# Keys of two tiles from centred rows, five more tiles transposed by DMA, and a new order of all instructions

## The chip, the cores and the metric

One Trainium2 chip, one of its cores. A core has TensorE (matmuls; in the profile PE, and its weight loads PEld), VectorE (DVE), ScalarE (ACT), GpSimd (POOL) and a queue for transfers, SyncE (SP). Each engine works through its own instructions in the order in which they were written; engines wait for each other through semaphores. The metric is the time of one execution on the device in microseconds (us); the kernel before takes 169.91 us, the median of three runs (169.8 to 170.13).

## The reference

A linear attention block and a feed-forward block, each behind a layer norm, on x of 2048 rows and 512 columns in bf16; 32 heads of 16 columns; the hidden layer of the second block has 1792 columns.

```python
phi = lambda t: where(t > 0, t + 1, exp(t)) + 1e-6
q, k, v = heads(layernorm(x) @ wqkv)
kv  = einsum("bhsd,bhse->bhde", phi(k), v)
z   = einsum("bhsd->bhd", phi(k))
o   = einsum("bhqd,bhde->bhqe", phi(q), kv) / (einsum("bhqd,bhd->bhq", phi(q), z) + 1e-6)
h   = x + o @ wo
out = h + relu(layernorm(h) @ w1) @ w2
```

The sum over all rows in kv and z is a barrier: no row of o can be had before every key is done.

## The kernel before

The 2048 rows are 16 tiles of 128 rows (t = 0 to 15), and four chunks c of four tiles. The whole program is one list of short words, `ORDER` (line 18): each word is a step, a call of the function `op_<word>` with the numbers behind the dots, and the steps are issued in the order of the list. An engine's own order is the order of its steps in the list, so a step that has to wait holds up everything behind it on its engine. PSUM is eight banks of 128x512 in f32 (`bk`), and each matmul step names the bank that it writes: it can't start before the readers of the bank's last content are done.

*Keys.* `lx` loads x. `S` and `A` take mean and variance of a tile on VectorE, `R` makes the reciprocal deviation on ScalarE (a logarithm and an exponential, lines 232 and 233), `N` normalises the tile on VectorE (line 251, into `ln_nat`, which is `h_nat`). The normalised tile must be transposed for the products: either on TensorE (`T`, line 270, four blocks of 128 columns into a bank, then copied to `lnT` by ScalarE, `E`, or VectorE, `V`), or by a DMA transpose from SP (`X`, line 291). `K` multiplies with wk, four matmuls over the contraction (line 299); `F` is the exponential and `U` the relu of the keys on ScalarE (lines 317 and 320, both from PSUM; one or two tiles at a time), `M` clips the exponential and adds 1e-6 (line 324), `D` adds both (line 327). `W` (line 332) stands for U and D together, on VectorE from PSUM. `G` (line 351) sums phi(k).T times normalised x over all tiles in banks 4 to 7; `za`, `zf` and `z` sum phi(k).

*Middle.* `zc`, `zh` make z ready, `gD` brings the sums out of banks 4 to 7, `kv`, `kx`, `m`, `mA` make from them, wv and wo one matrix for each head block. `Q`, `qF`, `qU`, `qM`, `qD` or `qW` are to queries what K to W are to keys, by chunk. `dn` (line 448) is the denominator, `dnl` and `dnx` (ScalarE) its reciprocal, spread over the columns of each head; `dt` (line 480) transposes it by DMA into `rd`, tile by tile, and `dm` (VectorE) multiplies the queries with it, a chunk at a time. There is a way on TensorE for that too, `rt` and `re`, not used in this list.

*Second half.* `h` (line 494) is o @ wo, `hD` adds x, `s` and `a` are the statistics, `r` the deviation, `n` centres the tile, `x` transposes it by DMA (`t` and `e` on TensorE and ScalarE), `p` (line 510) is the product with w1, `pA` and `pD` its relu on ScalarE and VectorE, `f` (line 530) the product with w2, `fo` (line 538) multiplies with the deviation and adds h, `fd` stores. The deviation of the second norm is applied at the very end, since relu passes a positive factor through. `warm` (line 215) issues dummy matmuls on zeros at the start. `lk`, `lq`, `lv`, `lo`, `l1`, `l2` load weights; `masks` makes constants on GpSimd. All transfers and DMA transposes go through SP.

Of the kernel before, what the change touches and what calls it, by code (L numbers as in the profile page):

```python
# [33 lines left out]
a.3 a.0 hD.2 qM.2.0.2 n.0 a.1 n.1 dm.1.0.2 dm.1.2.2 n.3 s.2 Q.3.2.0 Q.3.3.1 qD.2.0.2 a.2 qM.2.2.2 n.2 qF.3.0.2
qF.3.2.2 l2.3.4 x.0 qM.3.2.2 qD.2.2.2 h.5.6 h.7.7 h.6.5 x.1 t.2.3 r.0.4 e.2 h.4.4 x.3 dn.2.3 dnl.2 dnx.2.0.2
p.0.0.2 dt.8 hD.6 qM.3.0.2 qW.3.2.2 hD.4 p.0.1.3 qD.3.0.2 hD.5 dnx.2.2.2 pA.0.0.2 p.0.3.1 p.0.2.0 dn.3.6
pD.0.2.2 p.0.5.3 p.0.4.2 pD.0.4.2 p.0.7.1 p.0.6.0 p.0.13.3 s.6 dt.10 p.0.12.2 dt.11 dt.9 hD.7 a.6 s.5 dm.2.0.2
dm.2.2.2 dnl.3 pA.0.6.2 a.5 pD.0.12.2 f.2.6.0.7 s.7 h.11.7 h.9.0 p.0.9.3 h.8.5 p.0.8.2 dnx.3.2.2 dnx.3.0.2
# [542 lines left out]
```

## Time and profile before

| | |
|---|---|
| median of three runs | 169.91 us (169.8 to 170.13) |
| span of the profiled execution, first to last instruction | 168.6 us |
| TensorE busy | 163.1 us (97%), 875 matmuls |
| VectorE busy | 104.7 us (62%); 5.00 of 5 us in each slice from 10 to 25 us |
| ScalarE busy | 64.3 us (38%) |
| DMA | 15.36 MB, mean 91 GB/s; 16 engines over 90% busy between 5 and 10 us |

The profiled execution has no time of its own beside its span; the median lies 1.35 us above the span, which is what stands around the first and last instruction. A line `start duration engine line ...` of a timeline gives us from the start of the span. A line of groups gives, behind the count, the busy time and then the mean ns of one instruction. Matmuls are pipelined: a 128x512 matmul of bf16 is written down as 0.38 us, but the next one starts 0.216 us after it, so the end of a group is modelled. `[idle before <-releaser]` says how long the engine had idled and what ended it.

### The profile page before, as it was taken

The page shows a single profiled execution, that of the slowest core. Times are in us where ns is not written, and L with a number is a line of the kernel's source. Part 1 is how long each engine was busy: PE and PEld are TensorE (multiplying, and loading weights), DVE is VectorE, ACT ScalarE, POOL GpSimd, SP SyncE. Part 2 cuts the span into 40 slices and gives each one's busy share as a digit, 9 for nine tenths or more (in the row PEclk, how much of TensorE's full clock was granted, in tenths as well). Part 3 has the DMA queues.
Part 4 walks back from the last instruction along what each step waited for, and adds up shares of the span by engine and source line. Part 5 has one row for each costly group of instructions (what it writes and reads, how often), then busy time and mean ns, then how long its engine had stood idle before and what let it go on. Part 6 is the DMA issues. An engine that isn't in the chain of part 4 may idle for free.

```text
span 168.6 us, 2307 instructions
## 1 busy us (share of the span) xinstructions
PE 163.1 (97%) x875; PEld 76.3 (45%) x875; DVE 104.7 (62%) x207; ACT 64.3 (38%) x97; POOL 4.8 (3%) x21
## 2 busy tenths in 40 slices
...
DMA packets 30091, 15.36 MB, mean 91 GB/s; under 512 B 22656, under 2 KB 29056, under 8 KB 30080
## 3 DMA queue, kind: packets, MB, share of 16 engines
...
HBM read 7.86 MB, written 2.10 MB: 59 GB/s over the span
## 4 chain that ended last, share of the span: by engine, by line
PE 84%; ACT 4%; DMA 4%; SPq 3%; DVE 2%; issue 1%; DVEq 0%; ACTq 0%
PE bk L530 29%; PE bk L510 29%; PE bk L351 7%; PE bk L299 7%; PE bk L494 6%; PE bk L307 5%; DMA wk_sb<-in_A_wqkv_dram 3%; ACT eb L317 1%; DMA rd<-wk_sb 1%; SPq L201 1%; SPq L480 1%; PE bk L448 1%; ACT rb L320 1%; DVE pqT L332 1%; ACT lnT L280 1%
## 5 line engine op out<-in xcount | busy, mean ns | idle before, releaser
L530 PE MATMUL bk<-w_sb,at 128*128 128x512 bf16 (+2 forms) x252 | 51.5, 355 | 0.0
L510 PE MATMUL bk<-lnT,w_sb 128*128 128x512 bf16 x224 | 51.4, 379 | 0.0
L516 ACT ACTIVATE at<-bk 128x1024 bf16<-128x1024 f32 x14 | 14.1, 1023 | 70.3 <-PE bk L510 70.3
L521 DVE TENSOR_SCALAR at<-bk 128x1024 bf16<-128x1024 f32 x14 | 17.0, 1221 | 33.7 <-PE bk L510 33.7
L530 PEld LDWEIGHTS <-at 128*128 128x128 bf16 x252 | 23.6, 98 | 25.2
L510 PEld LDWEIGHTS <-w_sb 128*128 128x128 bf16 x224 | 21.8, 98 | 26.0 <-issue 0.2
L538 DVE SCALAR_TENSOR_TENSOR gT<-bk,rstd,h_nat 128x512 bf16<-128x512 f32 (+2 forms) x18 | 12.0, 686 | 18.3 <-PE bk L530 15.9
L317 ACT ACTIVATE eb<-bk 128x1024 bf16<-128x1024 f32 (+1 forms) x18 | 16.5, 925 | 6.1 <-PE bk L299 3.5
L299 PE MATMUL bk<-wk_sb,lnT 128*128 128x512 bf16 x64 | 15.5, 379 | 0.6 <-DMA wk_sb<-in_A_wqkv_dram 0.5
L494 PE MATMUL bk<-m_sb,pqs 128*128 128x512 bf16 x64 | 15.5, 379 | 0.1
L307 PE MATMUL bk<-lnT,wq_sb 128*128 128x512 bf16 x64 | 15.1, 379 | 0.1
L320 ACT ACTIVATE rb<-bk 128x1024 bf16<-128x1024 f32 (+1 forms) x15 | 13.6, 906 | 1.2 <-PE bk L307 1.2
L351 PE MATMUL bk<-at,h_nat 128*128 128x512 bf16 x56 | 13.7, 379 | 0.0
L500 DVE TENSOR_TENSOR h_nat<-bk,x_nat 128x512 bf16<-128x512 f32 x16 | 10.8, 678 | 2.7 <-PE bk L494 2.6
L226 DVE BATCH_NORM_STATS2 st<-x_nat 128x6 f32<-128x512 bf16 x16 | 10.6, 678 | 1.8 <-DMA x_nat<-in_A_x_dram 1.8
L228 DVE BATCH_NORM_STATS2 st<-h_nat 128x6 f32<-128x512 bf16 x16 | 10.5, 679 | 0.0
L299 PEld LDWEIGHTS <-lnT 128*128 128x128 bf16 x64 | 5.9, 98 | 8.2 <-ACT lnT L280 1.2
L494 PEld LDWEIGHTS <-pqs 128*128 128x128 bf16 x64 | 6.1, 98 | 7.9 <-DVE pqs L484 1.2
L307 PEld LDWEIGHTS <-wq_sb 128*128 128x128 bf16 x64 | 6.1, 97 | 7.3 <-issue 0.4
L351 PEld LDWEIGHTS <-h_nat 128*128 128x128 bf16 x64 | 6.0, 98 | 6.6
L461 ACT ACTIVATE wk_sb<-ld 128x1024 bf16<-128x1024 f32 x8 | 8.0, 1048 | 0.1
L324 DVE TENSOR_SCALAR eb<-eb 128x1024 bf16<-128x1024 bf16 (+1 forms) x18 | 6.9, 388 | 1.2 <-ACT eb L317 1.1
...
## 6 DMA issues: line engine op xcount, KB each, us to landing
...
```

Source lines behind the costliest of these rows:

```text
L299: nc.tensor.matmul(bk[:, b, :], lhsT=lnT[c][:, kd, j * P : (j + 1) * P], rhs=wk_sb[:, kd, :], start=(kd == 0), stop=(kd == KD - 1),)
L307: nc.tensor.matmul(bk[:, b, :], lhsT=wq_sb[:, kd, j * P : (j + 1) * P], rhs=lnT[c][:, kd, :], start=(kd == 0), stop=(kd == KD - 1),)
L317: nc.scalar.activation(out=buf(eb, kind, i, n), in_=bank(at_bank[kind, i], n), func=ACT.Exp)
L320: nc.scalar.activation(out=buf(rb, kind, i, n), in_=bank(at_bank[kind, i], n), func=ACT.Relu)
L351: nc.tensor.matmul(bk[:, KD + kd, :], lhsT=ln_nat[:, t, kd * P : (kd + 1) * P], rhs=pk(t)[:, 0, :], start=(t == 0), stop=(t == NT - 1),)
L494: nc.tensor.matmul(bk[:, b, :], lhsT=pqs[:, (c * KD + jb) % NQ, j * P : (j + 1) * P], rhs=m_sb[:, jb, :], start=(jb == 0), stop=(jb == KD ...
L500: nc.vector.tensor_tensor(out=h_nat[:, t : t + n, :], in0=bank(at_bank["h", t], n), in1=x_nat[:, t : t + n, :], op=ALU.add,)
L510: nc.tensor.matmul(bk[:, b, cols], lhsT=w1_sb[:, kd, f * P : (f + 1) * P], rhs=lnT[c][:, kd, cols], start=(kd == 0), stop=(kd == KD - 1),)
L516: nc.scalar.activation(out=acts[c % 2][:, f : f + n, :], in_=bank(at_bank["p", c, f], n), func=ACT.Relu)
L521: nc.vector.tensor_scalar(out=acts[c % 2][:, f : f + n, :], in0=bank(at_bank["p", c, f], n), scalar1=0.0, scalar2=None, op0=ALU.max,)
L530: nc.tensor.matmul(bk[:, b, 0 : w * P], lhsT=acts[c % 2][:, f, j * P : (j + 1) * P], rhs=w2_sb[:, f, k * P : (k + w) * P], start=(f == 0), ...
L538: nc.vector.scalar_tensor_tensor(out=o_t[:, t % NO, cols], in0=bk[:, at_bank["f", t, k], 0 : w * P], scalar=rstd2[:, t : t + 1], in1=h_nat ...
```

## The change

For tiles 0 and 2 the keys no longer start from the normalised tile. `C` subtracts the mean only, into a new buffer `xc`; `T` transposes that, into `xcT`; `K` multiplies it with wk; and the reciprocal deviation, one number for each row, is applied as the scale of the exponential and the relu (`scale_of`). `Nc` makes the normalised tile from `xc` later, for G and for the queries, and X transposes it by DMA. Tile 0 is transposed, copied and multiplied in two halves of the contraction (tile 2 is transposed in halves, and multiplied whole). `Na` normalises five tiles (1, 6, 7, 8, 13) on ScalarE in place of VectorE; it needs the product -mean x deviation, which `nm` makes on GpSimd. Seven N steps are left out (tiles 0, 1, 2, 6, 7, 8, 13). The tiles transposed by DMA go from nine to fourteen: 0, 1, 2, 5 and 6 come in. The relu and add of tiles 1, 3 and of 14, 15 become W on VectorE, those of the last two query products become U and D. One of the sixteen denominator tiles, tile 5, is transposed on TensorE (`rt.5`, `re.5`). There are seven dummy matmuls, eleven before; the first five transfers are x in place of x and wk mixed; two relu steps of the second half move from ScalarE to VectorE. The list of all steps is new. The change also adds two small constants and steps for another way to sum z (`zg`, `zhi`, `zlo`, `zs`), which the new list doesn't use.

The list at the places that matter, old then new, and the functions:

```diff
-const table lx.0.1 lx.2.1 S.0 lx.1.1 S.2 A.0 S.1 A.2 R.0.1 N.0 R.2.1 lx.3.1 lk.0.2 lx.4.2 masks warm.1.7
-warm.9.7 A.1 R.1.1 T.0.6 S.3 warm.1.7 N.2 T.2.4 N.1 A.3 E.0 R.3.1 T.1.5 lk.2.2 S.4 E.1 N.3 A.4 V.2 S.5 A.5
-K.0.6 lx.6.2 K.1.3 T.3.1 F.0.1 U.0.1 lx.8.4 E.3 K.2.0 M.0.1 S.6 D.0.1 K.3.2 A.6 S.7 F.1.1 M.1.1 lx.12.4 R.4.2
-N.5 A.7 N.4 U.1.1 D.1.1 F.2.1 U.2.1 R.6.2 S.8 S.9 N.7 A.9 A.8 M.2.1 N.6 lq.0.2 G.0 T.5.1 E.5 T.4.3 G.1 X.7
-K.5.1 D.2.1 E.4 K.4.0 R.8.2 T.6.3 G.2 N.9 X.9 F.3.1 U.3.1 S.12 N.8 S.13 X.8 lq.2.2 M.3.1 A.13 A.12 D.3.1 E.6
-K.6.2 F.4.2 R.12.2 U.4.2 K.7.3 G.3 M.4.2 S.11 F.6.2 U.6.2 N.12 D.4.2 S.10 S.14 N.13 M.6.2 A.11 A.10 D.6.2 A.14
-R.10.2 X.12 K.9.1 G.4 N.11 S.15 N.10 A.15 X.13 K.8.0 G.5 G.6 za.2 U.8.2 F.8.2 X.11 X.10 G.7 R.14.2 K.13.1
-K.12.0 M.8.2 N.15 D.8.2 za.4 N.14 K.11.3 K.10.2 G.8 l2.0.3 F.12.2 U.12.2 za.6 X.15 X.14 Q.0.0.0 F.10.2 Q.0.1.1
...
-z.1.2.14 z.3.2.14 qM.0.2.2 l2.7.3 lo.0.2 lo.2.2 l1.2.2 qM.0.0.2 qD.0.2.2 G.13 zc G.14 qD.0.0.2 zh dn.0.0 G.15
-gD.2.2 gD.0.2 Q.1.1.3 Q.1.0.2 dnl.0 dnx.0.0.2 Q.1.2.0 dnx.0.2.2 kv.3.4 kv.0.4 kv.1.4 kv.2.4 Q.1.3.1 qF.1.0.2
-qM.1.0.2 kx qF.1.2.2 qW.1.0.2 dt.0 dt.3 dt.2 dt.1 m.2.6 m.1.5 m.3.7 m.0.4 mA.0.2 Q.2.0.2 Q.2.1.3 qM.1.2.2
-mA.2.2 qW.1.2.2 dn.1.5 dm.0.0.2 dm.0.2.2 dnl.1 dnx.1.2.2 Q.2.3.1 h.3.5 hD.3 h.0.6 h.1.7 hD.0 s.3 dnx.1.0.2
...
-fo.14 fo.15.3.1 f.15.4.0.14.2.1 fd.12 fd.14 fd.15.3.1 fo.15.0.2 fo.15.2.1 fd.15.0.2 fd.15.2.1
+lx.0.1 const table lx.2.1 S.0 lx.3.1 S.2 lx.1.1 A.0 S.3 lx.4.2 R.0.1 A.2 C.0 lk.0.2 R.2.1 A.3 R.3.1 warm.7.6
+T.0.3.2.2 C.2 E.0.2.2 S.1 T.0.7.0.2 T.2.2.2.2 T.2.0.0.2 lk.2.2 N.3 A.1 S.5 T.3.6 lx.6.2 S.4 A.5 E.0.0.2 R.1.1
+E.2.0.2 A.4 nm.1.1 V.3 masks Nc.0 V.2.2.2 K.0.5.0.2 Na.1 K.0.5.2.2 R.4.2 K.2.7 N.5 N.4 F.0.1 M.0.1 lx.8.4 Nc.2
+X.1 K.3.2 X.5 T.4.3 U.0.1 D.0.1 F.2.1 U.2.1 lq.2.2 S.6 S.7 A.6 G.0 E.4 lx.12.4 A.7 S.8 M.2.1 F.3.1 X.2 K.4.0
+M.3.1 K.1.3 R.6.2 K.5.1 nm.6.1 D.2.1 Na.6 S.9 W.3.1 F.1.1 G.2 nm.7.1 M.1.1 A.8 X.6 A.9 Na.7 X.7 R.8.2 W.1.1 N.9
+S.10 X.9 S.12 S.13 G.3 A.12 A.13 nm.8.1 lq.0.2 F.4.2 Na.8 U.4.2 M.4.2 G.1 D.4.2 R.12.2 nm.13.1 K.6.2 X.8 K.7.3
+N.12 X.12 F.6.2 Na.13 S.11 S.14 A.11 M.6.2 U.6.2 K.9.1 S.15 A.14 A.10 D.6.2 G.4 G.5 R.10.2 A.15 K.8.0 K.12.2 G.6
+N.10 X.13 N.11 K.13.3 U.8.2 F.8.2 za.2 X.0 R.14.2 Q.0.1.1 X.10 M.8.2 N.14 D.8.2 X.11 U.12.2 F.12.2 Q.0.0.0 G.9
+qF.0.0.2 K.10.2 K.11.3 G.8 N.15 qU.0.0.2 X.15 X.14 K.14.0 K.15.1 F.10.2 za.4 za.6 M.12.2 za.8 D.12.2 M.10.2
...
+l1.0.2 lv.0.2 l2.3.4 G.10 W.14.2 G.7 G.11 zf.12 z.0.0.14 z.1.0.14 z.2.0.14 z.3.0.14 qU.0.2.2 qM.0.2.2 qD.0.0.2
+G.14 zc G.15 zh qD.0.2.2 dn.0.0 gD.0.2 Q.1.0.2 dnl.0 gD.2.2 dnx.0.0.2 Q.1.1.3 qF.1.0.2 kv.3.4 kv.2.4 kv.0.4
+kv.1.4 qM.1.0.2 kx Q.1.3.1 Q.1.2.0 dnx.0.2.2 m.0.4 m.3.7 m.1.5 qW.1.0.2 m.2.6 qF.1.2.2 mA.2.2 dt.1 Q.2.0.2
+Q.2.1.3 dt.0 mA.0.2 qM.1.2.2 dt.2 dt.3 qW.1.2.2 dm.0.0.2 Q.2.3.7 l2.7.3 l2.0.3 qF.2.0.2 dn.1.0 dm.0.2.2 dnl.1
+dnx.1.0.2 Q.2.2.6 h.1.0 h.0.4 Q.3.1.1 h.3.5 hD.1 s.1 dnx.1.2.2 hD.0 qU.2.2.2 a.1 qU.2.0.2 rt.5.4 s.0 qM.2.0.2
+Q.3.0.0 dt.4 re.5 hD.3 dt.6 a.0 dt.7 qF.2.2.2 qF.3.0.2 qU.3.0.2 n.1 n.0 s.3 a.3 Q.3.3.3 dm.1.0.2 h.2.4 Q.3.2.2
+qU.3.2.2 dm.1.2.2 qF.3.2.2 h.7.5 h.6.1 hD.2 n.3 h.5.4 x.1 x.0 s.2 x.3 a.2 qM.2.2.2 n.2 t.2.2 qD.2.2.2 h.4.0 e.2
...
+f.15.1.0.14.0.2 f.13.4.0.7 fd.11 f.14.7.0.7 f.15.5.0.14.3.1 f.13.4.7.7 fo.8 fd.8 f.14.7.7.7 f.12.0.0.7 fo.10
+fo.15.3.1 fo.15.0.2 fd.15.3.1 fd.10 fd.15.0.2 fo.14 fo.13 f.12.0.7.7 f.15.5.0.14.2.1 fd.14 fd.13 fo.12 fo.15.2.1
+fd.12 fd.15.2.1
@@ -84,6 +85,7 @@
     NE = 4
     NQ = 8
     NO = 4
+    HEAD = {0: 0, 2: 1}
 
     const = ctx.enter_context(tc.tile_pool(name="const", bufs=1))
     big = ctx.enter_context(tc.tile_pool(name="big", bufs=1))
@@ -135,6 +137,8 @@
     rb = big.tile([P, NE, 2, CW], BF16, name="rb")
     ld = big.tile([P, 2, CW], F32, name="ld")
     rd = big.tile([P, 4, CW], BF16, name="rd")
+    xc = big.tile([P, len(HEAD), D], BF16, name="xc")
+    xcT = big.tile([P, len(HEAD), KD, P], BF16, name="xcT")
     pqs = big.tile([P, NQ, CW], BF16, name="pqs")
     hn = big.tile([P, NQ, D], BF16, name="hn")
     o_t = gT
@@ -142,6 +146,9 @@
     rn = wk_sb
     z_acc = acts[1][:, 0:4, :].rearrange("p a n -> p (a n)").bitcast(F32).rearrange("p (a n) -> p a n", a=2)
     zeros = m_sb[:, 0, :]
+    ones32 = const.tile([P, Q4], BF16, name="ones32")
+    pick = const.tile([P, 1], BF16, name="pick")
+    zrow = acts[1][:, 4:6, :]
     bk = psum.tile([P, 8, CW], F32, name="bk")
 
     def pk(t, n=1):
@@ -175,6 +182,8 @@
         nc.vector.memset(eps5[:], 1e-5)
         nc.vector.memset(eps6[:], 1e-6)
         nc.vector.memset(ones[:], 1.0)
+        nc.vector.memset(ones32[:], 1.0)
+        nc.vector.memset(pick[:], 1.0 / Q4)
         make_identity(nc, ident[:])
 
     def keep(dst, rows, pattern, base, mult):
@@ -243,6 +252,18 @@
             scalar1=nmean[:, t : t + 1], scalar2=rstd[:, t : t + 1], op0=ALU.add, op1=ALU.mult,
         )
 
+    def op_nm(t, n):
+        nc.gpsimd.tensor_scalar(
+            out=nmean[:, t : t + n], in0=mv[:, t : t + n, 0], scalar1=rstd[:, t : t + 1], scalar2=-1.0,
+            op0=ALU.mult, op1=ALU.mult,
+        )
+
+    def op_Na(t):
+        nc.scalar.activation(
+            out=ln_nat[:, t, :], in_=x_nat[:, t, :], func=ACT.Identity,
+            bias=nmean[:, t : t + 1], scale=rstd[:, t : t + 1],
+        )
+
     op_R = lambda t, n: rstd_of(rstd[:, t : t + n], mv[:, t : t + n, 1])
     op_r = lambda t, n: rstd_of(rstd2[:, t : t + n], mv2[:, t : t + n, 1])
 
@@ -254,6 +275,18 @@
             op0=ALU.subtract, op1=ALU.mult,
         )
 
+    def op_C(t):
+        nc.vector.tensor_scalar(
+            out=xc[:, HEAD[t], :], in0=x_nat[:, t, :], scalar1=mv[:, t, 0:1], scalar2=None,
+            op0=ALU.subtract,
+        )
+
+    def op_Nc(t):
+        nc.vector.tensor_scalar(
+            out=ln_nat[:, t, :], in0=xc[:, HEAD[t], :], scalar1=rstd[:, t : t + 1], scalar2=None,
+            op0=ALU.mult,
+        )
+
     def op_n(t):
         nc.vector.tensor_scalar(
             out=hn[:, t % NQ, :], in0=h_nat[:, t, :], scalar1=mv2[:, t, 0:1], scalar2=None,
@@ -263,6 +296,9 @@
     def lnT_of(t, k=0, n=KD):
         c, j = divmod(t, CT)
         return lnT[c][:, k : k + n, j * P : (j + 1) * P]
+
+    def keys_in(t, k=0, n=KD):
+        return xcT[:, HEAD[t], k : k + n, :] if t in HEAD else lnT_of(t, k, n)
 
     def transpose(src, b, k, n):
         tp = bank16(b, n)
@@ -271,16 +307,18 @@
         return tp.rearrange("p (k n) -> p k n", k=n)
 
     def op_T(t, b, k=0, n=KD):
-        at_bank["T", t, k] = transpose(ln_nat[:, t, :], b, k, n)
+        at_bank["T", t, k] = transpose(
+            xc[:, HEAD[t], :] if t in HEAD else ln_nat[:, t, :], b, k, n
+        )
 
     def op_t(t, b):
         at_bank["t", t, 0] = transpose(hn[:, t % NQ, :], b, 0, KD)
 
     def op_E(t, k=0, n=KD):
-        nc.scalar.activation(out=lnT_of(t, k, n), in_=at_bank["T", t, k], func=ACT.Copy)
+        nc.scalar.activation(out=keys_in(t, k, n), in_=at_bank["T", t, k], func=ACT.Copy)
 
     def op_V(t, k=0, n=KD):
-        nc.vector.tensor_copy(out=lnT_of(t, k, n), in_=at_bank["T", t, k])
+        nc.vector.tensor_copy(out=keys_in(t, k, n), in_=at_bank["T", t, k])
 
     def op_e(t):
         nc.scalar.activation(out=lnT_of(t), in_=at_bank["t", t, 0], func=ACT.Copy)
@@ -293,11 +331,10 @@
 
 
     def op_K(t, b, k=0, n=KD):
-        c, j = divmod(t, CT)
         at_bank["k", t] = b
         for kd in range(k, k + n):
             nc.tensor.matmul(
-                bk[:, b, :], lhsT=lnT[c][:, kd, j * P : (j + 1) * P], rhs=wk_sb[:, kd, :],
+                bk[:, b, :], lhsT=keys_in(t, kd, 1)[:, 0, :], rhs=wk_sb[:, kd, :],
                 start=(kd == 0), stop=(kd == KD - 1),
             )
 
@@ -313,11 +350,18 @@
         u = unit[kind] + i
         return pool[:, u // 2 % NE, u % 2 : u % 2 + n, :]
 
+    def scale_of(kind, i):
+        return rstd[:, i : i + 1] if kind == "k" and i in HEAD else 1.0
+
     def exp_of(kind, i, n):
-        nc.scalar.activation(out=buf(eb, kind, i, n), in_=bank(at_bank[kind, i], n), func=ACT.Exp)
+        nc.scalar.activation(
+            out=buf(eb, kind, i, n), in_=bank(at_bank[kind, i], n), func=ACT.Exp, scale=scale_of(kind, i)
+        )
 
     def relu_of(kind, i, n):
-        nc.scalar.activation(out=buf(rb, kind, i, n), in_=bank(at_bank[kind, i], n), func=ACT.Relu)
+        nc.scalar.activation(
+            out=buf(rb, kind, i, n), in_=bank(at_bank[kind, i], n), func=ACT.Relu, scale=scale_of(kind, i)
+        )
 
     def min_of(kind, i, n):
         e = buf(eb, kind, i, n)
...
```

More of the change, by code (lines that the diff above doesn't have):

```diff
@@ L34 @@
[L34 to L38, printed above, removed]
@@ new lines @@
+x.7 x.4 dt.12 x.5 h.10.4 hD.10 f.0.3.0.7 f.3.2.0.7 x.6 s.10 pD.0.10.2 f.3.2.7.7 fo.3 h.9.5 hD.9 h.11.7 hD.11
+s.11 h.8.4 dm.3.0.2 hD.8 a.11 f.0.3.7.7 f.2.0.0.7 f.2.0.7.7 dm.3.2.2 h.14.1 h.13.5 fo.0 fo.2 n.11 p.1.12.2
+f.1.6.7.7 a.10 hD.13 hD.14 fo.1 p.1.5.1 p.1.13.3 h.12.6 p.1.4.0 pA.1.4.2 h.15.7 p.1.6.5 p.1.0.0 hD.12 hD.15 s.14
+s.8 p.1.7.6 a.8 a.14 s.9 s.12 fd.3 n.10 s.13 pD.1.12.2 a.9 p.1.1.1 p.1.11.4 r.4.4 a.13 pA.1.6.2 p.1.3.6 pA.1.0.2
+p.1.2.5 p.1.9.1 p.1.10.3 p.1.8.0 a.12 pD.1.2.2 s.15 pA.1.8.2 n.12 n.8 n.13 f.5.7.0.7 f.6.1.0.7 n.14 fd.2 x.11
```

44 lines of the change are left out of this document (28 added, 16 removed).

## The prediction

> **What bounds the kernel now.** I read the page's busy shares first, then the chain that ended last, then TensorE's timeline, to see where TensorE is not streaming.
>
> ```profile
> span 168.6 us, 2307 instructions
> PE 163.1 (97%) x875; PEld 76.3 (45%) x875; DVE 104.7 (62%) x207; ACT 64.3 (38%) x97; POOL 4.8 (3%) x21
> ```
> ```profile
> 3.65 4.42 DMA wk_sb<-in_A_wqkv_dram
> ...
> 8.11 0.61 PE bk L299 x2
> ...
> 15.65 0.22 PE bk L270 x4
> ...
> 155.22 10.66 PE bk L530 x77
> ...
> 165.91 0.35 DVE gT L538
> ```
> TensorE is busy from end to end. The chain enters it at 8.11, when the second half of wk has landed, and leaves it at 165.9. So the time is: the moment of 8.11, plus the matmul work left then, plus every gap in it, plus a tail of 168.56 - 165.88 = 2.7 us. Four 128-column transposes stream in 0.22, eight 512-column matmuls in 1.73 (16.57 to 18.30 below), 0.216 each.
>
> The gaps come from TensorE's timeline: a group's start minus (start before + its count x 0.216; a duration holds 0.16 of drain on top).
>
> ```profile
> 1.25 3.85 PE L215 MATMUL bk<-m_sb 128*128 128x512 bf16 x10 [1.25 <-DVE ones L177]
> 5.45 0.40 PE L270 MATMUL bk<-ident,h_nat 128*128 128x128 bf16 x4 [0.35 <-DVE h_nat L251]
> ...
> 6.45 0.71 PE L270 MATMUL bk<-ident,h_nat 128*128 128x128 bf16 x8 [0.38 <-DVE h_nat L251]
> 7.00 0.59 PE L299 MATMUL bk<-wk_sb,lnT 128*128 128x512 bf16 x2
> 8.11 1.46 PE L299 MATMUL bk<-wk_sb,lnT 128*128 128x512 bf16 x6 [0.52 <-DMA wk_sb<-in_A_wqkv_dram]
> ...
> 12.66 1.03 PE L351 MATMUL bk<-pk_lo,h_nat 128*128 128x512 bf16 x4
> 13.75 1.90 PE L299 MATMUL bk<-wk_sb,lnT 128*128 128x512 bf16 x8
> ...
> 16.57 1.89 PE L299 MATMUL bk<-wk_sb,lnT 128*128 128x512 bf16 x8
> 18.30 1.03 PE L351 MATMUL bk<-at,h_nat 128*128 128x512 bf16 x4
> ```
> ```profile
> 44.18 1.03 PE L307 MATMUL bk<-lnT,wq_sb 128*128 128x512 bf16 x4
> 45.13 1.04 PE L404 MATMUL bk<-wo_sb,kvbd 128*128 128x512 bf16 x4
> 46.26 1.89 PE L307 MATMUL bk<-lnT,wq_sb 128*128 128x512 bf16 x8
> ...
> 49.34 2.75 PE L494 MATMUL bk<-m_sb,pqs 128*128 128x512 bf16 x12
> ...
> 53.65 3.62 PE L307 MATMUL bk<-lnT,wq_sb 128*128 128x512 bf16 x16
> 57.34 2.94 PE L494 MATMUL bk<-m_sb,pqs 128*128 128x512 bf16 x12
> ```
> After 8.11: 0.22 before 13.75 (12.66 + 0.86 = 13.52), 0.09 before 45.13, 0.27 before 46.26, 0.23 before 57.34 and 0.19 within that group (2.94 against 2.75 for the same twelve); small ones elsewhere I put at 0.15. About 1.15 in all. That, the transposes and the 8.11 are all a new order can win.
>
> **The change, part by part.** *Transposes.* Before: seven tiles x 4 on TensorE (T) plus t.2, 32. After: T.0 and T.2 in halves, T.3, T.4, t.2 and rt.5, 24. Eight fewer x 0.055 = **-0.44**, certain, since TensorE has no cover. Five more tiles go through SP's DMA transposes (X: 9 to 14), and one denominator tile leaves it (dt: 16 to 15).
>
> *The head.* The point of a centred tile is that C.0 needs the mean only. But C.0 stands behind S.3 and A.2 on VectorE:
>
> ```profile
> 3.02 1.29 DVE L226 BATCH_NORM_STATS2 st<-x_nat 128x6 f32<-128x512 bf16 x2 [1.79 <-DMA x_nat<-in_A_x_dram]
> ...
> 4.30 0.66 DVE L226 BATCH_NORM_STATS2 st<-x_nat 128x6 f32<-128x512 bf16 x1
> 4.88 0.17 DVE L227 BATCH_NORM_AGGREGATE mv<-st 128x2 f32<-128x6 f32 x1
> 4.98 0.41 DVE L251 TENSOR_SCALAR h_nat<-x_nat,mv,rstd 128x512 bf16<-128x512 bf16 x1
> ```
> Starts step by about 0.08 less than the durations. C.0 starts at 4.97, where N.0 starts today: the first transpose comes at 5.39 against 5.45. T.2 comes at 5.73 and T.3 at 6.6. All that, with K.0's first half, is over by 7.5; the second half still waits for wk. SP issues lk.2 as its seventh transfer, as now, behind the same bytes, so again 8.11. Useful work done by then is equal (12 transposes, 2 matmuls). The head wins nothing before 8.11.
>
> After 8.11 I walked each queue with these rows:
>
> ```profile
> L280 ACT ACTIVATE lnT<-bk 128x512 bf16<-128x512 bf16 x6 | 3.4, 587 | 0.2 <-PE bk L270 0.2
> L320 ACT ACTIVATE rb<-bk 128x512 bf16<-128x512 f32 x4 | 2.4, 589 | 0.0
> L232 ACT ACTIVATE rstd<-mv,eps 128x1 f32<-128x1 f32 x4 | 1.2, 294 | 2.8 <-DVE mv L227 2.6
> L233 ACT ACTIVATE rstd<-rstd 128x1 f32<-128x1 f32 x4 | 0.8, 203 | 0.1
> L258 DVE TENSOR_SCALAR hn<-h_nat,mv 128x512 bf16<-128x512 bf16 x16 | 5.3, 345 | 0.1
> L327 DVE TENSOR_TENSOR pk_lo<-rb,eb 128x512 bf16<-128x512 bf16 x2 | 0.8, 414 | 0.0
> L332 DVE SCALAR_TENSOR_TENSOR pqT<-bk,eb 128x1024 bf16<-128x1024 f32 x3 | 3.7, 1219 | 0.1
> ```
> One per-partition operand costs ScalarE 0.09 (L232 against L233). So exponential and relu of tiles 0 and 2 go from 0.59 to 0.68, and a normalisation on ScalarE (Na, two such operands; not in this trace) I put at 0.59 + 0.18 = 0.77; bounds 0.59 and 0.95.
>
> ScalarE: R.1 ends at 7.2, Na.1 runs 7.5 to 8.27, R.4 to 8.7, F.0 from 8.74 (K.0 ends 8.54 and drains 0.16), then U.0, F.2, U.2 each 0.09 overlapped, E.4 from 11.10 to 11.69. TensorE: K.0 8.11, K.2 8.54, K.3 9.40, T.4 10.27, G.0 10.5, K.4 due at 11.4 but E.4 lets it go at 11.75: a gap of **0.35** in place of 0.22. Without the four 0.09 it would be none; with Na at 0.95 it is 0.5.
>
> VectorE gives seven normalisations away (7 x 0.33 stepped) and takes C and Nc twice each (0.345, L258's kind, stepped 0.27), three relu-adds from PSUM instead of adds (0.69 against 0.41 twice, 1.22 against 0.68) and half a copy: even within 0.4. It is full between 10 and 25, so it stays the feeder with the least room, but its walk reaches the end of the z sums at 36.9, TensorE the z matmuls at 37.6.
>
> SP pays for the five X:
>
> ```profile
> L291 SPq DMA_TRANSPOSE lnT<-h_nat x9: 1188/1199/1276, 14.0 to 27.4; - x9
> ...
> DMA to landing us min/median/max: 2.4/2.5/4.0
> ```
> 1.2 us of SP each and 2.5 to landing, in series. X.1 issues at 8.3 and X.5 at 9.5; behind them wait lq.2, lx.12 (ahead of every X now, issued about 11.2 then), X.2, X.6, X.7, X.9, lq.0, X.8. Landings against need: X.1 10.8 against K.1 at 12.6; X.5 12.0 against 13.5; X.6 15.9 against 17.8; X.9 18.4 against 18.7; X.8 20.3 against 21.2; X.14 29.4 against 29.8. lx.12 needs to be there by 16.1, when S.12 comes up on VectorE, and has 4.9 us. All hidden, X.9 and X.14 with only 0.3 to spare; for such near misses I charge **0.2**.
>
> ```profile
> 3.45 2.78 POOL L181 TENSOR_SCALAR_AFFINE_SELECT erep<-erep 32x128 bf16<-32x128 bf16 x8
> ```
> POOL: the five products -mean x deviation (nm) are new there. nm.1 waits for R.1 (7.2), and the masks, now queued behind it, end near 12.4 instead of 6.2, as they start at 7.4 instead of about 1.3; nm.6 waits for them, and Na.6 runs 12.6 to 13.4. That stays inside X.6's 1.9 of room. The mask readers come after 37 us.
>
> *The middle.* gD now follows G.15 with two query products between, not three: kv starts **0.13** late. kx is at 43.7, m has three products to cover it (now none of 0.09 and 0.27). h.1 waits for dt.3, fourth in SP's row from 41.4: 41.4 + 3 x 1.21 + 2.5 = 47.6, two products on VectorE, 49.05, TensorE free at 48.95: **0.1**. The next round needed four dt before and missed by 0.42; now tile 5 is transposed on TensorE (rt.5, +0.22, counted), three dt remain, and h.7 is due within 0.05. Gaps then: 0.35 + 0.2 + 0.13 + 0.1 + 0.05 = 0.83 against 1.15, **-0.32**. From 60 us on I checked each product's PSUM bank against its reader: smallest margin 0.3, no gap, as now.
>
> *The tail.* The last output piece is again 128 columns, but SP now has fo.12's full tile to issue just before it; issues take 0.33 to 0.58 there.
>
> ```profile
> L545 SPq DMA_DIRECT2D out_dram<-gT x18: 332/333/582, 99.7 to 166.3; - x18
> ```
> VectorE does the last piece 0.1 to 0.4 after fo.12, so **+0.08**, bounds 0 and 0.3.
>
> Sum: -0.44 - 0.32 + 0.08 = -0.68, a span of 167.88. The median of the runs, 169.91, is 1.35 above the profiled span; with that kept, **169.2**, -0.4%. A measurement of this kernel tells about 0.2% from no change.
>
> **The rivals.**
>
> *The clock falls back (slower).* The dummy matmuls go from eleven to seven. They step by 0.43 at first (3.85 for ten), so seven end at 4.25, and until 8.11 only three groups of transposes (0.4 each) and two matmuls (0.59) are left, 1.8 busy in 3.9 us.
>
> ```profile
> 4.40:7.78 3.38, 2.46 (x19) 1.04 (x17) 3.36 (x11) 2.81 (x10) 1.53 (x6) 1.00 0.94 301
> ...
> 164.79:168.20 3.41, 1.08 (x17) 0.88 (x15) 0.83 (x2) 0.00 (x0) 0.00 (x0) 1.00 0.28 77
> 168.20:168.60 0.40, 0.00 (x0) 0.00 (x0) 0.00 (x0) 0.00 (x0) 0.00 (x0) 0.50 0.00 0
> ```
> With 2.46 busy in such a stretch the granted clock stayed at 1.00; after one with 1.08 it was 0.50. 1.8 lies between; somewhere there it decides. If it falls (or is not granted), the dense work after 8.11 runs at half rate for about as long as the dummies did, 3.1 us: 1.55 lost, less the 0.35 gap that is then covered, 169.2 + 1.2 = 170.4. [...] I give it 0.2.
>
> *Late transposes.* One SP queue, and X.9 lands behind lx.12 and lq.2: at the longest landing in the row, 4.0, K.9 waits 1.2 and the time is 170.4; at half of that 169.8. The longest was a single one of nine, so 0.15.
>
> *No gap at all.* If Na and the scaled exponentials cost no more than today's, and the near misses hit, only 0.1 of gaps remain: 168.4 to 168.6. 0.17.
>
> *Nothing gained.* The five transposes come off TensorE but the time goes into the wait for E.4: that needs 0.8 more of ScalarE work before 11.7 than I count. Within the forecast's upper edge.
>
> **How the numbers follow.** Forecast 0.48, alone 168.8 to 169.6; clock 0.20, late transposes 0.15, no gap 0.17. Faster: nearly all of 0.48, 0.17: 0.63. Slower: most of the clock case and half of the late one: 0.25. Same: 0.12. The range leaves one tenth on each side: 168.3 to 170.6.
>
> **What would show it.** Right: first transposes at 5.4; second half of K.0 at 8.1; granted clock 1.00 from 8 on; 24 transposes; a gap of about 0.35 before K.4; kv 0.1 late; nothing over 0.1 after 60; last matmul near 165.1. Wrong: matmuls 0.43 apart after 8.1; K.6 to K.9 waiting for DMA; VectorE waiting for x_nat at S.12; a ScalarE normalisation over 0.95; a second table load.

## The result, and the profile after

The changed kernel takes **173.0 us**, the median of four runs (172.37 to 175.26), against 169.94 for the kernel before on the same chip: a ratio of **1.016**, 95% interval 1.0125 to 1.0194. It is slower by 1.6%; 169.2 was predicted, and the range ended at 170.6.

The profiled execution was the longest of the four (175.26), more than 1.5% above the fastest, and the ratios here and below leave such executions out. Its page, first the span, the busy shares and the granted clock in forty slices:

```profile
span 173.5 us, 2294 instructions
PE 163.8 (94%) x847; PEld 76.1 (44%) x863; DVE 108.3 (62%) x209; ACT 64.3 (37%) x97; POOL 6.8 (4%) x26
PEclk9958999999999999999999999999999999999999
```
TensorE is 3 points less busy, and in the third and fourth slice (8.7 to 17.3 us) the clock is not full. The chain that ended last shows where time was waited for (start, duration, what):

```profile
3.61 5.63 DMA wk_sb<-in_A_wqkv_dram
...
9.28 4.42 PE bk L336 x10
...
21.66 3.96 DMA lnT<-h_nat
...
25.67 1.90 PE bk L336 x8
...
51.30 2.49 DMA rd<-wk_sb
...
170.47 0.35 DVE gT L606
```
And TensorE's timeline, the rows that answer to those of before:

```profile
1.25 3.17 PE L224 MATMUL bk<-m_sb 128*128 128x512 bf16 x7 [1.25 <-DVE m_sb L181]
5.28 0.72 PE L306 MATMUL bk<-ident,xc 128*128 128x128 bf16 x8 [0.86 <-DVE xc L279]
...
9.28 2.72 PE L336 MATMUL bk<-wk_sb,xcT 128*128 128x512 bf16 x6 [1.62 <-DMA wk_sb<-in_A_wqkv_dram]
11.80 1.91 PE L336 MATMUL bk<-wk_sb,lnT 128*128 128x512 bf16 x4
...
25.67 1.90 PE L336 MATMUL bk<-wk_sb,lnT 128*128 128x512 bf16 x8 [0.69 <-DMA lnT<-h_nat]
...
54.66 2.07 PE L562 MATMUL bk<-m_sb,pqs 128*128 128x512 bf16 x8 [0.73 <-DVE pqs L552]
```
The first transposes come at 5.28, as forecast. The second half of wk lands at 9.24, not 8.11. From 9.28 six matmuls take 2.72, where 1.46 stood before: half rate. At 25.67 K.8 waits for a DMA transpose that was issued at 21.66; at 54.66 the first h product waits.

The granted clock of this trace is full from 4.49, half from 7.91 and full again from 14.73: its changes lie 3.42 and 6.82 us apart, one and two steps of 3.41. The windows between them, the second stretch in its two steps (start:end, length, PE busy, PEld, DVE, ACT, POOL, granted clock, DMA share, GB/s):

```profile
4.49:7.91 3.42, 1.71 (x14) 0.92 (x15) 3.42 (x13) 2.96 (x12) 0.61 (x3) 1.00 0.89 274
7.91:11.32 3.41, 2.04 (x5) 0.69 (x5) 1.93 (x8) 1.80 (x5) 2.90 (x11) 0.50 0.81 198
11.32:14.73 3.41, 3.41 (x12) 1.46 (x11) 2.99 (x9) 2.10 (x5) 1.13 (x4) 0.50 0.79 217
```
The trace's first record of the full clock is at 4.49, just after the dummies; it was gone at 7.91, after a window with 1.71 busy. The next window, 2.04 busy while it waited for wk, did not bring it back; after the next one, 3.41 busy, it was full. Two windows of half rate lie on the dense work.

### The profile page after: what moved, and what is told of

The parts are those of the page before. It is cut to its first block, busy times and chain, and to the rows that moved or that the text cites. A ratio compares the mean times of both kernels' runs of the same rounds, so it can differ in the third digit from the quotient of the medians.

```text
span 173.5 us, 2294 instructions
## 1 busy us (share of the span) xinstructions
PE 163.8 (94%) x847; PEld 76.1 (44%) x863; DVE 108.3 (62%) x209; ACT 64.3 (37%) x97; POOL 6.8 (4%) x26
## 4 chain that ended last, share of the span: by engine, by line
PE 84%; DMA 7%; ACT 3%; SPq 1%; issue 1%; DVE 1%; DVEq 0%; ACTq 0%
PE bk L598 28%; PE bk L578 28%; PE bk L562 8%; PE bk L336 7%; PE bk L344 6%; PE bk L395 6%; DMA wk_sb<-in_A_wqkv_dram 3%; DMA lnT<-h_nat 2%; DMA rd<-wk_sb 1%; SPq L210 1%; ACT eb L357 1%; ACT h_nat L262 1%; PE bk L516 1%; ACT m_sb L475 1%; PE bk L306 1%
## 5 line engine op out<-in xcount | busy, mean ns | idle before, releaser
L578 PE MATMUL bk<-lnT,w_sb 128*128 128x512 bf16 x218 | 49.8, 379 | 0.3
L598 PE MATMUL bk<-w_sb,at 128*128 128x512 bf16 (+2 forms) x248 | 49.8, 355 | 0.2
L584 ACT ACTIVATE at<-bk 128x1024 bf16<-128x1024 f32 x12 | 12.0, 1019 | 69.0 <-PE bk L578 69.0
L589 DVE TENSOR_SCALAR at<-bk 128x1024 bf16<-128x1024 f32 x16 | 19.3, 1218 | 12.9 <-PE bk L578 12.9
L357 ACT ACTIVATE eb<-bk 128x1024 bf16<-128x1024 f32 (+1 forms) x16 | 15.3, 970 | 5.3 <-PE bk L344 3.4
L336 PE MATMUL bk<-wk_sb,lnT 128*128 128x512 bf16 x55 | 14.3, 398 | 0.7 <-DMA lnT<-h_nat 0.7
L362 ACT ACTIVATE rb<-bk 128x1024 bf16<-128x1024 f32 x11 | 11.1, 1021 | 1.5 <-PE bk L336 1.4
L336 PEld LDWEIGHTS <-lnT 128*128 128x128 bf16 x56 | 5.4, 101 | 8.6 <-DMA lnT<-h_nat 2.2
```

The source lines that it names most:

```text
L336: nc.tensor.matmul(bk[:, b, :], lhsT=keys_in(t, kd, 1)[:, 0, :], rhs=wk_sb[:, kd, :], start=(kd == 0), stop=(kd == KD - 1),)
L357: nc.scalar.activation(out=buf(eb, kind, i, n), in_=bank(at_bank[kind, i], n), func=ACT.Exp, scale=scale_of(kind, i))
L362: nc.scalar.activation(out=buf(rb, kind, i, n), in_=bank(at_bank[kind, i], n), func=ACT.Relu, scale=scale_of(kind, i))
L578: nc.tensor.matmul(bk[:, b, cols], lhsT=w1_sb[:, kd, f * P : (f + 1) * P], rhs=lnT[c][:, kd, cols], start=(kd == 0), stop=(kd == KD - 1),)
L584: nc.scalar.activation(out=acts[c % 2][:, f : f + n, :], in_=bank(at_bank["p", c, f], n), func=ACT.Relu)
L589: nc.vector.tensor_scalar(out=acts[c % 2][:, f : f + n, :], in0=bank(at_bank["p", c, f], n), scalar1=0.0, scalar2=None, op0=ALU.max,)
```

## The experiments

Theory one: seven dummy matmuls are too few, the clock falls, and the key products run at half rate. Theory two: the DMA transposes come too late, tile 8's above all, since SP works through them in series. A third candidate was the later landing of wk. Every edit is in the list `ORDER`; the kernel before ran on the same chip each time (170.19 to 170.32).

### The changed kernel again

> The changed kernel once more, for a second trace. Clock theory (the granted clock is halved after 7.9 us because too few dummies are left): again a stretch after 8 us in which matmuls start 0.43 us apart, time 172.0 to 173.5. Transfer theory (wk lands late and the DMA transposes queue up): wk lands at 9.2 again, K.8 waits 0.8 for its transpose, matmuls after 8 us may be at full rate; 172.0 to 173.0.

Measured: 172.88 us (172.25 to 173.26), ratio 1.016 [1.0129, 1.0191]. Its profiled execution (172.54) stands near the median, with a span of 170.8, and I use it for the balance. Chain and clock windows of this trace:

```profile
7.09 0.60 PE bk L336 x2
...
7.74 3.89 PE bk L336 x10
...
19.22 3.80 DMA lnT<-h_nat
...
23.07 1.05 PE bk L336 x4
```
```profile
4.12:7.54 3.42, 1.79 (x15) 0.92 (x15) 3.42 (x12) 2.70 (x11) 0.25 (x2) 1.00 0.90 298
7.54:10.95 3.41, 3.37 (x9) 1.13 (x8) 3.40 (x12) 2.89 (x6) 2.94 (x11) 0.50 0.61 187
```
Here wk's second half was there in time (the chain names no transfer between 7.09 and 7.74), and still the clock was lost, after 1.79 busy. Worked out as in the prediction (starts, counts x 0.216), in us against the trace of before:

| term | us |
|---|---|
| eight transposes fewer | -0.44 |
| K.0's second half due at 7.52 (7.09 + 2 x 0.216), with no wait, not 8.11 | -0.59 |
| half rate up to 10.95: two groups 1.43 and 0.35 longer than their counts give | +1.78 |
| gaps: 0.31 at 19.77, 0.69 at 23.07 (K.8), 0.14, 0.23 at 32.09, 0.49 + 0.18 at 51.95 (h.1), 0.08; 2.12 against 1.10 | +1.02 |
| last matmul to end of span, 3.26 against 2.86 | +0.40 |
| sum | +2.17 |

The spans differ by 2.2. The medians (172.88 and 170.21) differ by 2.7: where a time and a span are both on record, the time stands 1.7 to 1.9 above the span (172.54 and 170.8 here), not 1.35, so the traced execution of before was about 0.4 slower than its median. The balance explains two traces, not the whole 2.7. In it, both theories have a part, and something else sits at the end.

### More dummies: the clock alone

```diff
-A.3 R.3.1 warm.7.6
+A.3 R.3.1 warm.10.1
-T.2.0.0.2 lk.2.2
+T.2.0.0.2 warm.3.1 lk.2.2
-K.0.5.0.2 Na.1
+K.0.5.0.2 warm.4.1 Na.1
```

> The changed kernel with 17 dummies in place of 7: ten at the start, three between the transposes of tiles 2 and 3, four behind the first half of K.0. Nothing else moves. Clock theory: the granted clock stays full from about 4.5 us on, matmuls 0.216 apart, time 1.5 to 3 us below the changed kernel, 169.5 to 171. Transfer theory: the clock is not the cost, wk still lands near 9.2, time within 0.4 of the changed kernel, 172 to 172.8.

Measured: 173.69 us (173.04 to 174.39), ratio 1.0198 [1.017, 1.0226]: not faster than the change. The clock did hold from 4.46 on, but K.8 then waited 2 us for its transpose. TensorE's timeline, the chain, and the two clock windows there:

```profile
24.29 2.99 PE L336 MATMUL bk<-wk_sb,lnT 128*128 128x512 bf16 x8 [2.01 <-DMA lnT<-h_nat]
```
```profile
18.97 5.28 DMA lnT<-h_nat
```
```profile
21.53:24.94 3.41, 1.40 (x7) 0.45 (x6) 3.18 (x8) 0.92 (x3) 0.00 (x0) 1.00 0.97 78
24.94:28.36 3.42, 3.42 (x9) 1.18 (x8) 0.77 (x3) 2.32 (x4) 0.00 (x0) 0.50 0.57 114
```
The wait left a window 1.40 busy, and the clock fell at 24.94 for a window of dense work. So the first loss came back at another place. Why the wait grew from 0.69 to 2.16 has two parts. TensorE was due at K.8 at 22.13, only 0.25 earlier than in the second trace of the change (22.38): of the 0.8 that it was ahead at 12 us, the rest had gone into gaps of 0.29 at 17.22 and 0.56 at 19.52, where the change had one of 0.31. That much the half rate had covered. The larger part is the transpose itself, which landed 1.2 later (24.25 against 23.02) although it was issued 0.25 earlier. And the lost window is not what makes this version slow: the three executions without a trace have a mean granted clock of 1.0 on record and took 173.04 to 173.84.

### wk's second half first

```diff
-lx.4.2 R.0.1 A.2 C.0 lk.0.2 R.2.1
+lk.0.2 R.0.1 A.2 C.0 lx.4.2 R.2.1
```

> The changed kernel with one transfer moved: the first half of wk ahead of tiles 4 and 5, as in the kernel before. Transfer theory: the second half of wk lands at 8.1 in place of 9.2, time 1.1 us lower, about 171.3. Clock theory alone: the clock still falls, matmuls still 0.43 apart after 8 us; the order of the two transfers does not change the bytes ahead of the second half, so wk lands where it did and the time stays within 0.4 of the changed kernel.

Measured: 172.59 us (172.25 to 172.60), ratio 1.014 [1.0119, 1.0161], which overlaps the change's own interval. (Its profiled execution had a mean granted clock of 0.56, 0.50 from 8.3 to 11.6 and 0.56 from 12 to 280 us, and took 288.72 us.) wk landed by 7.7 without this edit too, above. Its landing moves from run to run (by 7.7, 8.07, 8.67 and 9.24 in four traces), and this change of order shows no effect on the time.

### The kernel before with seven dummies

```diff
-masks warm.1.7
-warm.9.7 A.1
+masks warm.7.7
+A.1
-S.3 warm.1.7 N.2
+S.3 N.2
```

> The kernel before with seven dummies at the start in place of ten, and without the one between the transposes. Clock theory: 1.0 to 1.7 us slower than before, 170.9 to 171.6, with a half-clock stretch after 7.5 us. Its rival (dummies are of no account, since both kernels have over 3 us of them at the start): within 0.2 of before, 169.7 to 170.2.

Measured: 172.08 us (171.18 to 173.53), ratio 1.0125 [1.0063, 1.0187]. Nothing but four dummies is gone, and 1.9 us are lost (1.1 to 3.2 by the interval). TensorE's timeline:

```profile
1.25 3.17 PE L215 MATMUL bk<-m_sb 128*128 128x512 bf16 x7 [1.25 <-DVE ones L177]
...
7.54 3.09 PE L299 MATMUL bk<-wk_sb,lnT 128*128 128x512 bf16 x8
10.69 1.89 PE L299 MATMUL bk<-wk_sb,lnT 128*128 128x512 bf16 x8
```
Eight key matmuls take 3.09 and the next eight 1.89, with no wait between: the full clock came at 9.95 only, where the trace has its first record of it; the 2.92 from 7.54 to the transposes at 10.46 are 5.65 steps of 0.427 and 2.35 of 0.216, which puts the change there too. (The mean granted clock begins with that record, so it reads 1.0 for this trace: it tells a lost clock, not a late one. The spacing shows both.) So the runs show two ways to lose: the clock is granted early and taken back, as in the two traces of the change (4.49 to 7.91 and 4.12 to 7.54), or it comes late. This is the clearest of the runs: by the medians, the dummies alone are worth more than half of what the change lost.

### The loads away from between the transposes, alone and with the dummies

```diff
-M.0.1 lx.8.4 Nc.2
+M.0.1 lx.8.4 lx.12.4 Nc.2
-G.0 E.4 lx.12.4 A.7
+G.0 E.4 A.7
-lq.2.2 S.6
+lq.2.2 lq.0.2 S.6
-nm.8.1 lq.0.2 F.4.2
+nm.8.1 F.4.2
```

> The changed kernel with two loads moved forward on SP: tiles 12 to 15 ahead of the first DMA transpose, the first half of wq right behind the second half, so that no load stands before the transpose of tile 8. Queue theory (K.8 waits because its transpose stands behind a load): the transpose of tile 8 lands in 2.5 rather than 3.8 to 5.3 us and K.8 waits under 0.3; the half-clock stretch stays; 0.5 to 1 us less than the changed kernel, 171.5 to 172.3. Its rival (what the transpose waits for is the ScalarE chain before it, not the load): time and wait unchanged, 172.3 to 172.9.

> Both edits: 17 dummies and the two loads moved forward. If clock and load order are the two causes, and each hid the other: full clock from 4.5 us on, no wait over 0.5 before K.8, 169.6 to 170.6. Rival (ScalarE chain): K.8 still waits 1.5 to 2 us at about 23.5, 172.5 to 173.5, as with the dummies alone.

Measured: alone 173.0 us (172.58 to 174.15), ratio 1.0167 [1.0115, 1.022]; with the seventeen dummies 172.07 (171.39 to 172.61), ratio 1.0099 [1.0072, 1.0127]. So neither cure helps alone (173.69 and 173.0 against 172.88), and both together win 0.8. With the loads alone, K.8 did not wait in the trace, as the queue theory had it, but the half rate lasted to about 10.5, and the first h product waited longer (TensorE):

```profile
6.99 3.73 PE L336 MATMUL bk<-wk_sb,xcT 128*128 128x512 bf16 x8
10.53 1.05 PE L336 MATMUL bk<-wk_sb,lnT 128*128 128x512 bf16 x4
...
22.39 1.89 PE L336 MATMUL bk<-wk_sb,lnT 128*128 128x512 bf16 x8
...
51.99 2.07 PE L562 MATMUL bk<-m_sb,pqs 128*128 128x512 bf16 x8 [0.89 <-DVE pqs L552]
```
At K.8 this trace is 0.68 ahead of the second trace of the change (22.39 against 23.07); after the wait at 51.99 (1.05 by the counts, 0.49 there) it is 0.04 behind (51.99 against 51.95).

The load lq.0 (256 KB) stood just ahead of X.8 on SP, and X.8 landed late behind it: 3.80 and 3.96 in the two traces of the change, 5.28 with the dummies; without it 3.4 (alone) and this with the dummies (chain):

```profile
19.02 4.45 DMA lnT<-h_nat
```
So taking the load away shortens the landing by 0.4 to 0.9, and 0.9 to 2.0 above the 2.5 of the prediction remain. The traces show a pattern for the rest, not a cause: a fetch of instructions (queue q8, one packet of 0.02 MB) passes between 18 and 22 us, a stretch that X.8 fills for the most part, in three of the four traces with seventeen dummies and X.8 on SP (5.28, 4.45 and 4.43 to landing) and in the fourth, with the masks (5.23), none does; none passes in the first trace of the change while X.8 is under way, nor between 18 and 22 in the second or with the loads alone (3.96, 3.80, 3.4). One passes in the kernel before too, at a landing of 4.0.

The trace of before had shown a late landing at this place. Its longest landing, 4.0, is the transpose that stands right behind the same load (SP's timeline, and the landing of what was issued about 18.8); the next, 3.6, was issued at 25.75, right behind a load of `w_sb`:

```profile
17.99 0.57 SPq L204 DMA_DIRECT2D wq_sb<-in_A_wqkv_dram  x1
18.84 6.20 SPq L291 DMA_TRANSPOSE lnT<-h_nat  x4
```
```profile
lnT<-h_nat SPq DMA_TRANSPOSE x1, 4.0
```

### The masks early on GpSimd

```diff
-nm.1.1 V.3 masks Nc.0
+nm.1.1 V.3 Nc.0
-lx.4.2 R.0.1 A.2
+lx.4.2 masks R.0.1 A.2
```

> 17 dummies, and the masks on GpSimd ahead of the first product of mean and deviation, as early as in the kernel before; loads where the changed kernel has them. ScalarE chain: the normalisation of tile 6 starts at 12.6 in place of 13.6, the transpose of tile 8 is issued 0.9 sooner, K.8 starts 0.9 sooner than with the dummies alone, 172.4 to 173.0. Queue theory: the transpose still lands behind the load of wq, under 0.4 gained, 173.2 to 173.9.

> All three edits. If clock, loads and masks are each a part: 169.0 to 169.8, no gap over 0.3 before 40 us. If the masks do not matter: as with dummies and loads, within 0.3.

Measured: with the dummies 172.76 us (172.66 to 173.01), ratio 1.0145 [1.0109, 1.018]; with dummies and loads 171.65 (171.2 to 171.84), ratio 1.007 [1.0045, 1.0096]. By the medians faster by 0.9 and 0.4 than without the edit, but the intervals of both pairs overlap, and not by the way I had in mind. ScalarE's timeline and then GpSimd's, of the run with the dummies:

```profile
12.67 0.33 ACT L241 ACTIVATE rstd<-mv,eps 128x2 f32<-128x2 f32 x1
13.03 0.20 ACT L242 ACTIVATE rstd<-rstd 128x2 f32<-128x2 f32 x1
13.95 0.81 ACT L262 ACTIVATE h_nat<-x_nat,nmean,rstd 128x512 bf16<-128x512 bf16 x1 [0.71 <-POOL nmean L256]
```
```profile
13.33 0.82 POOL L256 TENSOR_SCALAR nmean<-mv,rstd 128x1 f32<-128x1 f32 x2 [5.67 <-DVE eb L368]
```
GpSimd had been idle for 5.67 us, and Na.6 starts at 13.95, as late as in the change (13.85 in its second trace). What sets it here is the deviation of tile 6: R.6 stands on ScalarE behind F.2, U.2, E.4 and F.3 and ends at 13.2. In the trace with the dummies alone it was otherwise (ScalarE, then GpSimd):

```profile
12.40 0.20 ACT L242 ACTIVATE rstd<-rstd 128x2 f32<-128x2 f32 x1
```
```profile
13.06 0.74 POOL L256 TENSOR_SCALAR nmean<-mv,rstd 128x1 f32<-128x1 f32 x2
```
There R.6 was ready at 12.6, and the masks held GpSimd up to 12.96. So early masks would have gained some 0.4; but in the trace with the edit the full clock came at 6.9 and not at 4.46, and ScalarE's first exponential started 0.65 later (9.43 against 8.78), which takes the gain back. The two traces differ in the clock as well as in the edit. X.8 was issued at 19.32, and K.8 waited 2.12, as without this edit. What differs later is where the windows fall, counted in steps of 3.41 from the first record at 6.9:

```profile
20.55:23.96 3.41, 2.09 (x10) 0.76 (x8) 3.41 (x12) 2.24 (x5) 0.00 (x0) 1.00 1.44 140
23.96:27.37 3.41, 2.72 (x12) 1.29 (x14) 1.10 (x1) 1.70 (x2) 0.00 (x0) 1.00 0.57 115
```
The same wait is split over two windows here, 2.09 and 2.72 busy, and the clock holds. That does not explain the 0.9, since three of the four executions with dummies alone held it too and took 173.04 to 173.84; where the 0.9 and the 0.4 come from stays open.

### Tile 8 on TensorE

On top of dummies, loads and masks:

```diff
-K.6.2 X.8 K.7.3
+K.6.2 K.7.3 T.8.0
-N.12 X.12 F.6.2
+N.12 X.12 E.8 F.6.2
-K.8.0 K.12.2 G.6
+K.8.0 G.6 K.12.2
```

> Dummies, loads and masks as in the run before this one, and tile 8 transposed on TensorE and copied by ScalarE, with G.6 between K.8 and K.12. If the wait before K.8 (0.7) is the late landing of that one DMA transpose: K.8 does not wait, 0.4 to 0.8 less than with the three edits, 170.8 to 171.3. If the ScalarE chain to the normalisation of tile 8 is the bound: the same gap stands before T.8 or K.8, 171.4 to 171.9.

Measured: 171.53 us (170.95 to 172.65), ratio 1.0074 [1.0044, 1.0103], within the last one's interval. K.8 no longer waits; four more transposes (0.22) and a wait of G.6 for VectorE take most of what K.8's 0.70 had cost:

```profile
23.68 1.02 PE L395 MATMUL bk<-at,h_nat 128*128 128x512 bf16 x4 [0.24 <-DVE at L371]
```

### Towards a version that beats both

Twelve dummies (9, 2, 1) for seventeen, once with E.4 ahead of F.2, once with E.4 left and the last stores in the order of before (fd.12 ahead, fd.15's two halves last):

```diff
-U.0.1 D.0.1 F.2.1 U.2.1
+U.0.1 D.0.1 E.4 F.2.1 U.2.1
-G.0 E.4 lx.12.4
+G.0
```

> As tensor8, but with 12 dummies (nine, two, one) instead of 17, and the copy of tile 4 on ScalarE ahead of tile 2's exponential. If the 17 dummies held up the second half of K.0 where the clock came late, and the copy of tile 4 is what K.4 waits for: K.0's second half at 8.1 to 8.5, no 0.5 before K.4, 169.7 to 170.5, level with the kernel before. If 12 dummies are too few: half clock after 7 us, 171.5 or more.

> As tensor8, with 12 dummies in place of 17 (nine, two, one) and the last products in another order: the full tile 12 is finished and stored early, the pieces of tile 15 come last, as in the kernel before. If the dummies hold up the second half of K.0 (8.7 in tensor8) and the store of a whole tile right before the last piece lengthens the tail (3.0 to 3.1 us from the last TensorE work, 2.65 before): K.0's second half at 8.0 to 8.3, tail 2.7, together about 1 us less than tensor8, 170.2 to 170.8, level with the kernel before or slightly above. If neither: 171.3 to 171.8.

Measured: with E.4 early 171.69 us (171.4 to 173.26), ratio 1.0102 [1.0034, 1.017]; without, 171.15 (170.69 to 171.58), ratio 1.0039 [1.0019, 1.0058], the best of the changed orders and still slower than before. E.4 early pushes U.2 back, whose bank G.0 needs (TensorE's timeline of the first, below); in the other K.2's second half waits at 9.19 for VectorE's copy, and the last output piece comes at 166.84 in a span of 169.8, 2.96 apart (its timeline, and its chain):

```profile
12.40 0.38 PE L395 MATMUL bk<-pk_lo,h_nat 128*128 128x512 bf16 x1 [1.00 <-ACT rb L362]
```
```profile
9.19 0.60 PE L336 MATMUL bk<-wk_sb,xcT 128*128 128x512 bf16 x2 [0.24 <-DVE xcT L321]
```
```profile
166.84 0.35 DVE gT L606
```
Its gaps from 9 us on sum to about 2.3, the largest 0.41 there, 0.41 at G.6 (23.44), 0.39 at 26.42, where the profile names no releaser, and 0.28 before K.4, against 1.1 before; with tile 8's four transposes added, only 0.22 of the 0.44 saved stands against that. The tail did not come back with the old order of the stores, so that order is not its cause.

### One part alone on the kernel before

Tile 5's denominator on TensorE, the one part of the change that I tried in the old list by itself (the centred tiles and the normalisation on ScalarE were not):

```diff
-dt.4 dt.7 dt.5 qF.2.0.2
+dt.4 dt.7 qF.2.0.2
-qU.2.0.2 h.2.6
+qU.2.0.2 h.2.6 rt.5.4 re.5
```

> The kernel before, with the denominator of tile 5 transposed on TensorE as in the change, and nothing else. Own theory: the gap of 0.42 at the fourth group of h falls under 0.1 and four transposes cost 0.22, so 0.1 to 0.3 less than before. Rival (the copy on ScalarE holds up the exponentials behind it): gap moves to the query products, time unchanged or up to 0.4 more.

Measured: 171.09 us (170.5 to 172.26), ratio 1.0053 [1.0021, 1.0084]. ScalarE's re.5 waits for the transposes, and the exponential and relu behind it come late (ScalarE, then TensorE):

```profile
54.66 0.60 ACT L472 ACTIVATE rd<-bk 128x512 bf16<-128x512 bf16 x1 [1.20 <-PE bk L270]
```
```profile
57.15 1.89 PE L307 MATMUL bk<-lnT,wq_sb 128*128 128x512 bf16 x8 [0.79 <-ACT rb L320]
```
The old gap before h.7 is gone and a larger one stands before the third chunk's query product: at this place in the old list the part loses by itself. The second half of wk let TensorE go on 0.6 later in this run (8.71), so not all of the 0.9 is shown to be that wait.

## Why the prediction was wrong, point by point

- **What bounds the kernel: right.** TensorE's entry, its gaps and the tail give the time; the balance above closes to 0.1 with these terms alone.
- **Transposes, -0.44: right,** and so were the durations taken for new operations. The groups of the page's kind in the trace after:

```profile
L262 ACT ACTIVATE h_nat<-x_nat,nmean,rstd 128x512 bf16<-128x512 bf16 x5 | 4.0, 807 | 0.6 <-POOL nmean L256 0.5
L357 ACT ACTIVATE eb<-bk,rstd 128x512 bf16<-128x512 f32 x2 | 1.4, 687 | 2.0 <-PE bk L336 2.0
```
  Na 0.807 (0.77 taken), scaled exponential 0.687 (0.68).
- **The head: half right.** The first transposes came at 5.28 and 5.35 (5.39). "So again 8.11" was wrong: wk landed at 9.24 in one trace and by 7.7 in the other. One trace of before could not show that this landing varies.
- **The clock: the step that failed most.** The sum gave it nothing. I saw the danger, gave it 0.2 and priced it at 1.2. The clock was lost in both traces of the change after windows half busy (1.71 and 1.79 of 3.41), and in two other traces with seven dummies (the kernel before with seven, and the loads alone) it was granted only at 9.95 and 10.57, the case that I had put in brackets, "or is not granted". The bracket I had, kept at 2.46 busy and lost at 1.08, was right, and so was the 1.8 that I counted for the change; it lies in the middle of the bracket, and 0.2 had no row behind it: it was my estimate. The runs now show 1.79 lost and 2.09 kept. The price for one window, 1.55, was near: 1.78 in the second trace. It was short for two: 2.7 in the first (1.22, 0.84, 0.21 and 0.41 beyond the counts of the four groups from 9.28 on). Of the eight executions of the change only the two traced ones and one more have a mean granted clock below 0.995 on record; whether the clock came late in the other five is not known.
- **The gap of 0.35 before K.4:** hidden behind half rate in the change; 0.28 where the clock is full (the best version, at 12.10). Right.
- **"That stays inside X.6's 1.9 of room": wrong twice.** I let Na.6 start when the masks ended, 12.6. In the second trace it started at 13.85, behind R.6, which the half rate had made late (ready at 13.39, masks done at 13.01). With the clock full, in the run with the dummies, R.6 was ready at 12.6, but the masks ended at 12.96 and nm.6 stood between, so that Na.6 started at 13.60. And I looked at X.6's own reader only. In the second trace X.6, X.7, X.9, lq.0 and X.8 follow on SP without a break, so X.8 takes over the whole delay: issued 1.4 later than the walk's 17.8. SP's timeline there:

```profile
14.69 3.82 SPq L329 DMA_TRANSPOSE lnT<-h_nat  x3
18.55 0.57 SPq L213 DMA_DIRECT2D wq_sb<-in_A_wqkv_dram  x1
19.22 1.19 SPq L329 DMA_TRANSPOSE lnT<-h_nat  x1
```
- **X.8's landing at 20.3: wrong by another 1.3,** as 2.5 was taken for every transpose of the row. It took 3.80, and landed at 23.0: 20.3 + 1.4 + 1.3. The late transposes were a rival with 0.15, named at K.9 and not at K.8, and as "a single one of nine"; which one it was, and what stood ahead of it, was not asked.
- **The rivals were priced as if one excluded the other.** They came together. Why the single cures gained nothing is seen in one trace each: with the dummies, part of what the head won went into waits for transposes and tile 8's transpose landed 1.2 later besides; with the loads, what K.8 won was lost again at h.1.
- **kv 0.13, h.1 0.1, h.7 0.05:** kv and h.7 show no gap; h.1 waited 0.49 + 0.18 and 0.89 + 0.18 in the traces of the change, and at most 0.06 + 0.18 with more than seven dummies (the best version). The place was right and the size was not: of the four transposes "x 1.21" the second held SP 2.35 in the first trace of the change, where the four took 6.21, and about 1.9 in the second by my estimate (5.78 for the four, less three and the pauses of the first). Why is not shown.
- **From 60 us on nothing over 0.1: right.** The largest in the second trace is 0.08, at 61.93.
- **The tail, +0.08 with 0.3 as its bound: wrong,** +0.40. The last stores' order was not it. What the traces show is that SP's closing wait on the stores is 1.2 long and single in the changed kernels, 0.9 in two pieces before. From the end of SP's last issue to the end of that wait it is 1.2 in both. But SP passes five closing semaphores, 0.06 us apart when it need not wait: before, the last of the five is the one that ends the wait; in the change it is the first, and the other four follow, so 0.25 of the 0.40 stands behind the wait. Why their order differs stays open.

What stays open: why the best version, with clock and K.8 mended, has twice the small gaps of before (waits of 0.1 to 0.4, most on VectorE and ScalarE, that I did not take apart one by one), why X.8 lands late without a load ahead of it, and the tail.
